# Output banks added up in memory by transfers, and spread between the last chunks of a stage

## The chip, the cores and the metric

The kernel runs on one NeuronCore of a Trainium2 chip. The core has five engines that run at the same time, each its own list of instructions in order: TensorE multiplies matrices (PE in the profile, PEld for its loads of weights), VectorE (DVE), ScalarE (ACT) and GpSimd (POOL) work element by element, and SyncE (SP) starts transfers between the chip's memory and the on-chip memory. Sixteen DMA engines carry these transfers. TensorE writes its results into eight PSUM banks of 128 partitions by 512 floats, and a bank is free again when another engine has read it. The metric is the device time of one execution in microseconds (us). Before the change the median of three runs is 953.04 us (951.15 to 953.58).

## The reference

A windowed attention (4 batches, 8 heads, 576 positions, each looking at 64 positions) makes 2304 tokens of 512 numbers; two gated layers follow. In the second, which the change touches, both factors are linear:

```
x = attention(q, k, v)                          # 2304 x 512
x = (sigmoid(x @ w_gate) * (x @ w_val)) @ w_out   # 512 -> 1536 -> 512
a, b = x @ w_a, x @ w_b                         # 2304 x 1536 each
out = (a * b) @ w_out2                          # 2304 x 512
```

The weights come as 64-bit floats; the result is 32-bit.

## The kernel before, in words

Tokens go in nine blocks of 256. The hidden width of 1536 goes in twelve chunks of 128 (`fc` from 0 to 11). Every factor of a product is kept as a high and a low part, and a product is three matmuls: high by high, high by low, low by high.

The stage around the change is the second layer for tokens 0 to 1279, from about 375 to 580 us; it is followed by the first layer for tokens 1280 to 2303. Tokens 256 to 1279 are a group of four blocks. For each chunk `quad` (L915, with its matmuls in `multiply`, L849) computes both factors by seven products instead of eight, whose sums ScalarE keeps as `r` (L868) and VectorE adds (L871); VectorE then multiplies the factors (L881), and ScalarE and VectorE split the result into `hh` and `hl` or the two parts of `h` (L481, L483). Block 0, tokens 0 to 255, is computed plainly, chunk by chunk, by `hidden` (L507, matmuls L472): chunks 0 to 5 during the stage, 9 to 11 at its end, 6 to 8 later. Its own output is added up by `projection` (matmuls L525, VectorE's add L597).

After every second chunk, a *pair*, `row_banks` (L1106) makes the output of the four blocks: eight banks of 128 tokens by 512 columns (name `accq`, matmuls L987), each the sum of 12 matmuls with one PSUM bank. Six pairs make 48 banks of work. The first pair's banks are copied by ScalarE into four tiles `resf` on chip (L989), those of the other five are added to these by VectorE (L991), and with the last pair SyncE writes the result (L1122). PSUM has two banks for this (`ps_acc`), so the third bank of work waits until the first has been read.

The banks aren't made at once: each is a job in a list `rest`, and `fill(n)` runs the next n jobs. During a quad some jobs run between the products; at the stage's end `fill(3)` and `fill(len(rest))` stand behind block 0's three chunks. A scheduler then orders each engine's instructions by an estimate of its own, within the dependencies and some that are put in by hand (`in_order`, `paced`).

Beside this run two more streams. Weights of the coming chunks are decoded from 64-bit words (L373 to L401 on ScalarE, VectorE and GpSimd), combined for the seven products by GpSimd (`s`, `wq`, L422, L430), and saved to memory by SyncE (`ka`, `kb`, `ko`, L365, and `kq`, L432). At the end the operands of the next stage are loaded back (`xq`, from `bx`, L1193) and split by ScalarE (`op`, L797) and VectorE (L798, with sums L805), and its first weights are loaded (`wf`, L830) and combined by GpSimd (L450, L453).

Of the kernel before, what the change touches and what calls it, by code (L numbers as in the profile page):

```python
# [10 lines left out]
F32 = mybir.dt.float32  # L11
# [4 lines left out]
ALU = mybir.AluOpType  # L16
# [5 lines left out]
def tile_window_attention_gated_mlps(ctx, tc, q, k, v, w1g, w1v, w1o, w2a, w2b, w2o, out):  # L22
    nc = tc.nc
# [3 lines left out]
    P = 128  # L27
# [1074 lines left out]
    def fill(n=1):  # L1102
        for _ in range(min(n, len(rest))):
            rest.pop(0)()

    def row_banks(res, hs, rows, begin, end):  # L1106


        banks = []
        for i in range(2 * NP):  # L1110
            j, sl = i // NP, slice(i % NP * P, (i % NP + 1) * P)
            cols = (slice(0, CH), slice(CH, W)) if end and rows[0] > N and i == 2 * NP - 1 else (slice(0, W),)
            r0 = rows[j] + i % NP * P
            for c in cols:
                pairs = [(h[j][a][:, sl], o[b][:, c]) for o, h in hs for a, b in ((0, 0), (0, 1), (1, 0))]
                banks.append((pairs, res[i // 2][:, i % 2, c], out[r0:r0 + P, c]))
        for pairs, d, to in banks:

            def job(d=d, p=pairs, b=begin, to=to):
                bank_sum(d, p, b)  # L1120
                if end:
                    nc.sync.dma_start(out=to, in_=d)  # L1122

            rest.append(job)
        return banks

    x_ops = next(built)
    fill(len(rest))
    x_ops = next(built)
# [15 lines left out]
                    i, at, mybir.DependencyInfo(mybir.DependencyClass.NoSync, mybir.DependencyReason.DATA), reason="paced"  # L1145
                )

    hs, h0s, res = [], [], None
    seconds = (
        lambda: late["hs"].tile([P, 2, W], F32R, tag="hs", name="h1"),  # L1150
        lambda: wts.tile([P, 2, DM], F32R, tag="wa", name="h1"),
# [2 lines left out]
    for fc in range(NF):  # L1154
        alone = ALONE.get(fc, ())
        for i, f0 in enumerate(alone):
            need(NF + f0, NEVER)
            w = parts[NF + f0]
            h0s.append((w, hidden(1, w, x[1, (0,)])))
            fill(2)  # L1160
            if i == len(alone) - 1:
                rest.append(lambda a=(1, 0, h0s, fc == 0, False): projection(*a))
                h0s = []
        need(NF + fc, NEVER)
        if fc == NF - 1:
            eased = len(nc.cur_bb.bb.instructions)
        limit[0] = min(NW - 1, NF + fc + 2)
        if fc == 0:
            res = [accp.tile([P, 2, W], F32, tag="xacc", name=f"resf{i}") for i in range(4)]
        w = parts[NF + fc]  # L1170
        g = [tmp.tile([P, W], F32, tag="hr", name=f"g{i}") for i in range(2)]
        counts = ((0, 0, 1, 1, 1, 1, 0), (0, 0, 1, 1, 1, 1, 0)) if len(rest) <= 4 else ((0, 1, 1, 1, 1, 1, 1), (0, 1, 1, 1, 1, 1, 1))
        extra = max(0, len(rest) - sum(counts[0]))

        def between(i):
            fill(counts[0][i] + (extra if i == 4 else 0))
            for _ in range(((0, 0, 0, 0, 2, 2, 2) if fc == 0 else (1, 1, 1, 0, 1, 1, 1))[i]):
                paced()

        hs.append((w["o"], quad(1, w, x_ops, between, g, seconds[fc % 3], lambda: None)))  # L1180
        if len(hs) == PAIR:
            fill(len(rest))
            row_banks(res, hs, (3 * N, N), fc == PAIR - 1, fc == NF - 1)
            hs = []
    late.clear()
    middle.close()
# [9 lines left out]
    for fc in BETWEEN:  # L1196
        h0s.append((parts[NF + fc], hidden(1, parts[NF + fc], x[1, (0,)])))
        x_ops = next(built)
    in_order(eased, (mybir.EngineType.DVE,))
    rest.append(lambda a=(1, 0, h0s, False, False): projection(*a))  # L1200
    steps = [(0, fc) for fc in range(NF)] + [(None, fc) for fc in LATER] + [(1, fc) for fc in range(NF)]
    fetched = []
# [1 line left out]
    def ahead(n):  # L1204
        while len(fetched) <= min(n, len(steps) - 1):
            ph, fc = steps[len(fetched)]
            fetched.append(fetch((1 if ph is None else ph) * NF + fc, ph is None))

    tied = len(nc.cur_bb.bb.instructions)
    ahead(0)  # L1210
    fill(3)
    whole(built)
    fill(len(rest))
    SLOTS = {4: (1, 0, 1, 0, 1, 1, 0), 7: (0, 1, 1, 1, 2, 1, 1)}

    def slots(number, first=False):
# [126 lines left out]
```

## Time and profile before

| | us |
|---|---|
| median of three runs | 953.04 |
| the profiled execution | 955.45 |
| its span, first to last instruction | 953.5 |
| TensorE busy in the span | 925.9 |
| VectorE busy | 708.4 |
| ScalarE busy | 478.8 |
| GpSimd busy | 303.3 |

Busy times are shares of one span, and engines work side by side, so they aren't added. The time is set by the chain of waits that ended last, and an engine's idle time counts only where that chain runs through it. In the rows below, `<-` behind an instruction in brackets names what ended the idle time before it; a name on the left of `<-` is what is written, on the right what is read.

### The profile page before, as it was taken

To read this page: it belongs to the slowest core of one execution; us is meant where nothing else is said; L and a number is where in the kernel's file an instruction comes from. 1 tells how busy PE (TensorE), PEld (TensorE's weight loads), DVE (VectorE), ACT (ScalarE), POOL (GpSimd) and SP (SyncE) were. 2 spreads that over 40 slices of the span, in tenths; PEclk is the share of its full clock that TensorE was granted. 3 is DMA by queue.
4 is the path that set the end of the run, shared out by engine and by line. 5 is a ranking of instruction groups with operands and counts; after the bars stand their busy time and mean duration, and the time that the engine had idled before them with its cause. 6 is when DMAs were issued, how large, how long until landed. Compare 5 with 4: busy or idle time off the path is not lost.

```text
span 953.5 us, 15652 instructions
## 1 busy us (share of the span) xinstructions
PE 925.9 (97%) x5504; PEld 773.1 (81%) x5504; DVE 708.4 (74%) x1379; ACT 478.8 (50%) x1063; POOL 303.3 (32%) x321
## 2 busy tenths in 40 slices
PE   7899999999999999999999989999999999999998
PEld 6698888887887788778877777788888888888886
DVE  6998787786569799788999875778788773354445
ACT  7897555686744456564555534655444243211111
POOL 4543222343226714362655336544430000000000
PEclk9999999999999999999999999999999999999999
DMA  8987598988568626565877566354547675554212
GB/s 203 237 237 221 197 326 291 336 286 245 153 220 310 225 109 220 195 220 178 269 236 261 210 198 222 111 188 158 158 150 220 198 275 153 159 173 134 89 66 88
DMA packets 144685, 193.69 MB, mean 203 GB/s; under 512 B 63584, under 2 KB 98912, under 8 KB 143968
## 3 DMA queue, kind: packets, MB, share of 16 engines
q1 hardware_dynamic: 144608, 192.71, 62.5%
q8 instruction: 43, 0.70, 0.3%
q14 instruction: 34, 0.28, 0.1%
HBM read 118.75 MB, written 69.47 MB: 197 GB/s over the span
## 4 chain that ended last, share of the span: by engine, by line
PE 69%; DVE 14%; DMA 5%; POOL 4%; ACT 4%; issue 3%; SPq 0%; DVEq 0%; POOLq 0%; ACTq 0%
PE qa L849 16%; PE accq L987 11%; PE qb L849 8%; PE gps L472 7%; PE vps L472 6%; PE accm L573 6%; PE qc L849 4%; PE accy L950 3%; PE accx L950 2%; DVE ex L392 2%; DVE wi L382 2%; PE xps L228 2%; DVE wi L379 1%; DVE wi L386 1%; DMA st_o<-in_moe_w_out_dram 1%
## 5 line engine op out<-in xcount | busy, mean ns | idle before, releaser
L849 PE MATMUL qa<-op,wq 128*128 128x512 f32 x432 | 112.9, 391 | 2.7 <-ACT r L868 2.3
L849 PE MATMUL qb<-op,wq 128*128 128x512 f32 x432 | 110.7, 390 | 0.9 <-POOL wq L430 0.6
L868 ACT ACTIVATE r<-qa 128x512 f32<-128x512 f32 x108 | 62.5, 594 | 90.0 <-PE qa L849 88.8
L472 PE MATMUL vps<-xh,wb 128*128 128x256 f32 (+1 forms) x392 | 105.6, 338 | 0.2 <-ACT hr L496 0.2
L472 PE MATMUL gps<-xh,wa 128*128 128x256 f32 (+1 forms) x392 | 105.2, 338 | 0.0
L849 PEld LDWEIGHTS qa<-op,wq 128*128 128x128 f32 x432 | 80.9, 188 | 20.4 <-ACT r L868 3.0
L849 PEld LDWEIGHTS qb<-op,wq 128*128 128x128 f32 x432 | 81.0, 188 | 18.4 <-POOL wq L430 1.0
L573 PE MATMUL accm<-hh,wo 128*128 128x512 f32 (+1 forms) x296 | 85.6, 357 | 1.6 <-DVE gacc L550 1.3
L386 POOL TENSOR_TENSOR wi<-wi,low 128x512 int32<-128x512 int32 x36 | 50.1, 1393 | 113.2 <-DVE wi L382 78.3
L472 PEld LDWEIGHTS gps<-xh,wa 128*128 128x128 f32 x392 | 69.2, 191 | 8.5 <-DVE hl L483 0.3
L472 PEld LDWEIGHTS vps<-xh,wb 128*128 128x128 f32 x392 | 69.0, 190 | 8.0 <-ACT hr L496 0.4
L987 PE MATMUL accq<-wo,h 128*128 128x512 f32 (+1 forms) x300 | 71.2, 382 | 3.8 <-DVE resf L991 3.7
L987 PEld LDWEIGHTS accq<-wo,h 128*128 128x128 f32 x300 | 54.8, 188 | 15.8 <-DVE resf L991 4.7
L472 PE MATMUL gps<-xl,wa 128*128 128x256 f32 (+1 forms) x196 | 65.9, 336 | 0.5 <-DVE xl L237 0.5
L472 PE MATMUL vps<-xl,wb 128*128 128x256 f32 (+1 forms) x196 | 65.7, 335 | 0.0
L392 DVE SCALAR_TENSOR_TENSOR ex<-ex,wi 128x512 f32<-128x512 f32 x72 | 53.3, 741 | 14.6 <-ACT ex L376 7.4
L481 ACT ACTIVATE hh<-qa 128x512 fp32r<-128x512 f32 x36 | 21.5, 597 | 84.4 <-DVE qa L881 55.5
L573 PEld LDWEIGHTS accm<-hh,wo 128*128 128x128 f32 x296 | 52.9, 189 | 11.9 <-DVE gacc L550 4.0
L987 PE MATMUL accq<-wo,hh 128*128 128x512 f32 x184 | 56.3, 397 | 1.5 <-ACT hh L481 1.4
L849 PE MATMUL qa<-op,wb 128*128 128x512 f32 x216 | 55.2, 391 | 1.9 <-ACT r L868 1.9
L849 PE MATMUL qc<-op,wa 128*128 128x512 f32 x216 | 56.9, 390 | 0.0
L189 ACT ACTIVATE pr<-pr,stat 128x128 f32<-128x128 f32 x144 | 54.0, 391 | 5.4 <-DVE stat L183 5.2
(180 smaller groups left out, 2154.9 us busy)
## 6 DMA issues: line engine op xcount, KB each, us to landing
wo<-ko SPq DMA_DIRECT2D x27, 512.0 KB, 4.2
wa<-ka SPq DMA_DIRECT2D x27, 512.0 KB, 4.4
st_o<-in_moe_w_out_dram SPq DMA_DIRECT2D x24, 512.0 KB, 5.0
ka<-wa SPq DMA_DIRECT2D x24, 512.0 KB, 5.4
kb<-wb SPq DMA_DIRECT2D x24, 512.0 KB, 3.9
ko<-wo SPq DMA_DIRECT2D x24, 512.0 KB, 5.1
kq<-wq SPq DMA_DIRECT2D x48, 256.0 KB, 4.5
wq<-kq SPq DMA_DIRECT2D x48, 256.0 KB, 3.2
```

What stands on the lines that cost most here:

```text
L189: nc.scalar.activation(out=pr[e][:, j, :], in_=pr[e][:, j, :], func=AF.Exp, bias=nmax[:, e, j:j + 1], scale=-1.0, accum_out=None if t in O ...
L228: nc.tensor.matmul(xps[dims, j, rows], lhsT=vv[:, 2 * j + e, :], rhs=pt[e][:, j, rows], start=True, stop=True)
L382: nc.vector.scalar_tensor_tensor(out=wi, in0=w1, scalar=-(1 << 30), in1=wi, op0=ALU.bitwise_and, op1=ALU.bitwise_or)
L386: (nc.vector if F >= NF else nc.gpsimd).tensor_tensor(out=wi, in0=wi, in1=low, op=ALU.add)
L392: nc.vector.scalar_tensor_tensor(out=wf, in0=wf, scalar=SMALLEST, in1=wi.bitcast(F32), op0=ALU.is_ge, op1=ALU.mult)
L472: nc.tensor.matmul(ps, lhsT=a[:, c * P:(c + 1) * P], rhs=b[:, c, :], start=(n == 0), stop=(n == 3 * NP - 1))
L481: nc.scalar.activation(out=hh, in_=hr, func=AF.Copy, scale=factor)
L573: nc.tensor.matmul(ps[:, m], lhsT=a[:, sl], rhs=b, start=k == 0, stop=k == total - 1)
L849: nc.tensor.matmul(ps, lhsT=a[:, c * P:(c + 1) * P], rhs=b[:, c, :], start=first and n == 0, stop=n == 5, skip_group_check=True,)
L868: nc.scalar.activation(out=r[n], in_=ps, func=AF.Copy)
L950: nc.tensor.matmul(bank[k], lhsT=a[n][i][:, sl], rhs=b[n][j], start=start and m == 0, stop=m == 2, skip_group_check=True,)
L987: nc.tensor.matmul(ps, lhsT=a, rhs=b, start=n == 0, stop=n == len(pairs) - 1)
```

## The change

The banks of tokens 256 to 1279 are no longer added up on chip. A new function `added_rows` takes the place of `row_banks` in this stage: ScalarE copies each bank into half of a tile `added`, of which a ring of buffers is used, and each full tile (256 tokens by 512 columns) is sent to the output. For the first pair SyncE writes it; for the other five GpSimd issues a transfer that adds it to what stands in memory. A tile is sent when the next tile's first bank has been multiplied, and the last one as a job of its own. VectorE's adds and the writes at the end are gone.

At the stage's end three jobs follow each of block 0's chunks 9, 10 and 11, and the rest comes ahead of the remaining operands of the next stage.

```diff
@@ -1124,6 +1124,41 @@
             rest.append(job)
         return banks
 
+    def added_rows(hs, rows, begin):
+
+
+        for i in range(2 * NP):
+            j, sl = i // NP, slice(i % NP * P, (i % NP + 1) * P)
+            pairs = [(h[j][a][:, sl], o[b]) for o, h in hs for a, b in ((0, 0), (0, 1), (1, 0))]
+            r0 = rows[j] + (i % NP - 1) * P
+
+            def job(i=i, p=pairs, to=out[r0:r0 + 2 * P].rearrange("(a p) f -> p a f", p=P) if i % 2 else None):
+                if i % 2 == 0:
+                    added[0] = accp.tile([P, 2, W], F32, tag="xacc", name="added")
+                bank_sum(added[0][:, i % 2], p, True)
+                if i % 2 == 0 and unsent:
+                    unsent.pop()()
+                if i % 2:
+                    unsent.append(lambda t=added[0]: send(t, to, begin))
+
+            rest.append(job)
+        rest.append(lambda: unsent.pop()())
+
+    unsent = []
+
+    def send(t, to, begin):
+        if begin:
+            nc.sync.dma_start(out=to, in_=t)
+        else:
+            at = next(i.name for i in reversed(nc.cur_bb.bb.instructions) if i.engine == mybir.EngineType.PE)
+            since = len(nc.cur_bb.bb.instructions)
+            nc.gpsimd.dma_start(out=to, in_=t, accum_op=ALU.add)
+            for i in nc.cur_bb.bb.instructions[since:]:
+                tc.add_manual_dep(
+                    i, at, mybir.DependencyInfo(mybir.DependencyClass.NoSync, mybir.DependencyReason.DATA), reason="send"
+                )
+
+    added = [None]
     x_ops = next(built)
     fill(len(rest))
     x_ops = next(built)
@@ -1145,7 +1180,7 @@
                     i, at, mybir.DependencyInfo(mybir.DependencyClass.NoSync, mybir.DependencyReason.DATA), reason="paced"
                 )
 
-    hs, h0s, res = [], [], None
+    hs, h0s = [], []
     seconds = (
         lambda: late["hs"].tile([P, 2, W], F32R, tag="hs", name="h1"),
         lambda: wts.tile([P, 2, DM], F32R, tag="wa", name="h1"),
@@ -1165,8 +1200,6 @@
         if fc == NF - 1:
             eased = len(nc.cur_bb.bb.instructions)
         limit[0] = min(NW - 1, NF + fc + 2)
-        if fc == 0:
-            res = [accp.tile([P, 2, W], F32, tag="xacc", name=f"resf{i}") for i in range(4)]
         w = parts[NF + fc]
         g = [tmp.tile([P, W], F32, tag="hr", name=f"g{i}") for i in range(2)]
         counts = ((0, 0, 1, 1, 1, 1, 0), (0, 0, 1, 1, 1, 1, 0)) if len(rest) <= 4 else ((0, 1, 1, 1, 1, 1, 1), (0, 1, 1, 1, 1, 1, 1))
@@ -1180,7 +1213,7 @@
         hs.append((w["o"], quad(1, w, x_ops, between, g, seconds[fc % 3], lambda: None)))
         if len(hs) == PAIR:
             fill(len(rest))
-            row_banks(res, hs, (3 * N, N), fc == PAIR - 1, fc == NF - 1)
+            added_rows(hs, (3 * N, N), fc == PAIR - 1)
             hs = []
     late.clear()
     middle.close()
@@ -1196,7 +1229,7 @@
     for fc in BETWEEN:
         h0s.append((parts[NF + fc], hidden(1, parts[NF + fc], x[1, (0,)])))
         x_ops = next(built)
-    in_order(eased, (mybir.EngineType.DVE,))
+        fill((3,3,3)[fc - BETWEEN[0]])
     rest.append(lambda a=(1, 0, h0s, False, False): projection(*a))
     steps = [(0, fc) for fc in range(NF)] + [(None, fc) for fc in LATER] + [(1, fc) for fc in range(NF)]
     fetched = []
@@ -1206,11 +1239,11 @@
             ph, fc = steps[len(fetched)]
             fetched.append(fetch((1 if ph is None else ph) * NF + fc, ph is None))
 
+    in_order(eased, (mybir.EngineType.DVE,))
     tied = len(nc.cur_bb.bb.instructions)
     ahead(0)
-    fill(3)
+    fill(len(rest))
     whole(built)
-    fill(len(rest))
     SLOTS = {4: (1, 0, 1, 0, 1, 1, 0), 7: (0, 1, 1, 1, 2, 1, 1)}
 
     def slots(number, first=False):
```

TensorE's order at the stage's end. `accq` is a bank of the last pair, `gps` and `vps` are the two factors of a plain chunk of block 0, and `acc` is its projection. Before:

```order
L472 MATMUL vps_6919<-xh1_0_4715,wb_6513 128x256
L987 MATMUL accq_6990<-wo_6422,hh_6698 128x512 x2
L987 MATMUL accq_6990<-wo_6422,hl_6699 128x512
L987 MATMUL accq_6990<-wo_6566,hh_6779 128x512 x2
L987 MATMUL accq_6990<-wo_6566,hl_6780 128x512
L987 MATMUL accq_7007<-wo_6422,hh_6698 128x512 x2
L987 MATMUL accq_7007<-wo_6422,hl_6699 128x512
L987 MATMUL accq_7007<-wo_6566,hh_6779 128x512 x2
L987 MATMUL accq_7007<-wo_6566,hl_6780 128x512
L987 MATMUL accq_7016<-wo_6422,h1_6726 128x512 x3
L987 MATMUL accq_7016<-wo_6566,h1_6791 128x512 x3
```

After, at the second and third of block 0's chunks:

```order
L472 MATMUL vps_6944<-xh1_0_4715,wb_6348 128x256
L987 MATMUL accq_6969<-wo_6457,hh_6741 128x512 x2
L987 MATMUL accq_6969<-wo_6457,hl_6742 128x512
L987 MATMUL accq_6969<-wo_6594,hh_6815 128x512 x2
L987 MATMUL accq_6969<-wo_6594,hl_6816 128x512
L472 MATMUL gps_6995<-xh1_0_4715,wa_6522 128x256
L472 MATMUL gps_6995<-xl1_0_4716,wa_6522 128x256
L472 MATMUL gps_6995<-xh1_0_4715,wa_6522 128x256 x2
L472 MATMUL gps_6995<-xl1_0_4716,wa_6522 128x256
L472 MATMUL gps_6995<-xh1_0_4715,wa_6522 128x256 x2
L472 MATMUL gps_6995<-xl1_0_4716,wa_6522 128x256
L987 MATMUL accq_6978<-wo_6457,h1_6762 128x512 x3
```

Six banks stood behind the last chunk before, one after the other; now two stand ahead of the first chunk, three singly between the chunks, and three behind the last.

SyncE's order of transfers near the end of the weight decoding. `xq` are the operands of the next stage, `k...` are saves of weights of chunks 10 and 11. Before:

```order
L365 DMA ko22_231<-wo_6422 128x1024
L365 DMA ka23_233<-wa_6494 128x1024
L1193 DMA xq01_6820<-bx1_140 128x1024
L1193 DMA xq00_6816<-bx0_139 128x1024
L365 DMA kb23_234<-wb_6513 128x1024
L432 DMA kq11_263<-wq5_6549 128x512
L432 DMA kq11_263<-wq6_6551 128x512
L1193 DMA xq11_6822<-bx1_140 128x1024
```

After:

```order
L432 DMA kq11_263<-wq5_6577 128x512
L432 DMA kq11_263<-wq6_6579 128x512
L432 DMA kq11_263<-wq7_6581 128x512
L432 DMA kq11_263<-wq3_6583 128x512
L365 DMA ko23_235<-wo_6594 128x1024
L1226 DMA xq01_6856<-bx1_140 128x1024
L1226 DMA xq00_6852<-bx0_139 128x1024
L1226 DMA xq11_6858<-bx1_140 128x1024
L1226 DMA xq10_6854<-bx0_139 128x1024
```

The four loads of `xq` stood between the last saves, the first two of them ahead of `kb23`; now all four stand behind the last save, `ko23`.

GpSimd's order from the last decoded weight to the first sums of the next stage, after:

```order
L401 TENSOR_TENSOR wo<-ex,wo 128x512
L1155 DMA out_dram<-added 128x2x512 x5
L450 TENSOR_TENSOR s_7060<-wf 128x256
L450 TENSOR_TENSOR s_7065<-s_7060,wf 128x256
L450 TENSOR_TENSOR s_7070<-wf 128x256
```

Before, L450 came directly behind L401; now five issues of adding transfers stand between them.

## Rows read from the trace of the kernel before

**Rows 1.** Page, busy time of each engine (us, share of the span, instructions)

```profile
PE 925.9 (97%) x5504; PEld 773.1 (81%) x5504; DVE 708.4 (74%) x1379; ACT 478.8 (50%) x1063; POOL 303.3 (32%) x321
```

**Rows 2.** Windows: stretch, length, busy per engine, clock, DMA share, GB/s

```profile
434.00:577.00 143.00, 137.11 (x642) 112.77 (x641) 129.03 (x196) 72.20 (x136) 63.88 (x68) 1.00 0.65 219
```

**Rows 3.** Windows of 20 us, same columns

```profile
520.00:540.00 20.00, 18.85 (x81) 14.67 (x81) 19.06 (x29) 10.63 (x21) 9.82 (x10) 1.00 0.70 245
540.00:560.00 20.00, 20.00 (x108) 17.33 (x107) 15.14 (x22) 5.80 (x9) 0.00 (x0) 1.00 0.47 166
560.00:580.00 20.00, 15.73 (x88) 12.86 (x88) 15.40 (x20) 7.83 (x16) 14.74 (x16) 1.00 0.59 203
```

**Rows 4.** Waits of PE, 434 to 600: us in total, times, longest us

```profile
PE accq L987 <- DVE resf L991: 3.7, 2, 2.5
PE qa L849 <- ACT r L868: 1.4, 2, 0.7
PE qb L849 <- POOL wq L430: 0.6, 1, 0.6
PE qa L849 <- DVE g L871: 0.6, 1, 0.6
PE accq L987 <- ACT hh L481: 0.6, 1, 0.6
PE acc L525 <- DVE resf L991: 0.4, 1, 0.4
PE qb L849 <- DVE hl L483: 0.3, 1, 0.3
PE vps L472 <- ACT hr L496: 0.2, 1, 0.2
```

**Rows 5.** Timeline of PE: start, us, instruction [idle before]

```profile
569.85 4.41 PE L987 MATMUL accq<-wo,h 128*128 128x512 f32 x18 [2.48 <-DVE resf L991]
...
575.45 1.70 PE L987 MATMUL accq<-wo,h 128*128 128x256 f32 x12 [1.20 <-DVE resf L991]
...
577.55 0.73 PE L525 MATMUL acc<-wo,hh 128*128 128x512 f32 x2 [0.40 <-DVE resf L991]
```

**Rows 6.** Groups by line, 375 to 625: count, busy, mean ns, idle before

```profile
L991 DVE TENSOR_TENSOR resf<-accq,resf 128x512 f32<-128x512 f32 (+1 forms) x41 | 26.7, 667 | 2.1 <-PE accq L987 2.0
...
L401 POOL TENSOR_TENSOR wo<-ex,wo 128x512 fp32r<-128x512 f32 x10 | 13.6, 1361 | 20.3 <-ACT wo L398 20.2
...
L989 ACT ACTIVATE resf<-accq 128x512 f32<-128x512 f32 x8 | 4.6, 594 | 2.8 <-PE accq L987 2.8
```

**Rows 7.** Timelines of ACT and PE around 545 us

```profile
544.38 1.06 ACT L797 ACTIVATE op<-xq 128x1024 fp32r<-128x1024 f32 x1 [3.54 <-DMA xq<-bx]
...
547.20 1.52 PE L849 MATMUL qa<-op,wb 128*128 128x512 f32 x6
```

**Rows 8.** Timeline of SP's issues, and the landing of xq

```profile
537.87 0.38 SPq L1193 DMA_DIRECT2D xq<-bx  x1
...
539.97 0.32 SPq L365 DMA_DIRECT2D ko<-wo  x1
...
DMA to landing us min/median/max: 3.8/5.9/6.8
```

**Rows 9.** Timeline of POOL, 530 to 574 us

```profile
530.05 0.74 POOL L422 TENSOR_TENSOR s<-ex 128x256 f32<-128x256 f32 x1 [7.45 <-DVE ex L392]
...
561.41 0.73 POOL L450 TENSOR_TENSOR s<-wf 128x256 f32<-128x256 f32 x1 [21.47 <-DMA wf<-kf]
...
573.67 4.08 POOL L453 TENSOR_TENSOR wq<-s,wq 128x256 fp32r<-128x256 f32 x3
```

**Rows 10.** Page, DMA queue of SP: packets, MB, share of 16 engines

```profile
q1 hardware_dynamic: 144608, 192.71, 62.5%
```

**Rows 11.** Timeline of DVE at the stage's end

```profile
577.75 1.77 DVE L805 TENSOR_TENSOR t<-xq,t 128x1024 f32<-128x1024 f32 x1
```

## The prediction

> **What bounds the kernel now.** I read the page's busy shares first: TensorE works 97% of the span and its clock is at the full 2.4 GHz almost throughout, so only its idle time can be won [rows 1]. Next the windows over the stage that the change touches. From 434 to 577 us, in which all but the last few of the adds that it removes run, TensorE is idle 143 − 137.1 = 5.9 us, while VectorE is busy 129.0 of 143, ScalarE 72.2, GpSimd 63.9 and the DMA engines 0.65 [rows 2]. By pieces, TensorE's largest hole is from 560 to 580: 4.3 of 20 us [rows 3]. Then the waits of TensorE alone: from 434 to 600 they sum to 7.8 us, of which 3.7 + 0.4 are for VectorE's add of an output bank, four waits of 0.3 to 0.6 (2.1 together) come before 555 us, and 1.4 us belongs to the next stage [rows 4]. The timeline shows the 4.1 us one by one: 2.48, 1.20 and 0.40 us, all while the last banks wait for a free PSUM bank, which VectorE gives back only after its adds, and those stand behind preparing the next stage's operands [rows 5]. So the stage is bound by TensorE, with VectorE close to full beside it, and at its end by VectorE.
>
> **The change, part by part.**
>
> *Removed: VectorE's adds.* 41 instructions (40 banks, one of them in two halves), 26.7 us in all, go from VectorE [rows 6]. This stands beside TensorE's work except at the end, where it makes the 4.1 us of waits. There banks now stand between block 0's chunks, so they are no longer crowded behind them, and each needs only a ScalarE copy. I take all three waits as gone. The last bank, whole again, takes a third of the 4.41 us of three whole ones, 1.47, for the 1.70 of its twelve half-width matmuls [rows 5]: 0.2 us. Sum: −4.3 us; bounds 0 (another wait takes their place) to −4.3.
>
> *Earlier in the stage* the four waits of 2.1 us (for g, for hl, for hh and for wq) are each for a result that is VectorE's or depends on its decoding [rows 4]. With 26 of its 129 us gone, some of them end sooner; which ones the trace doesn't say. I take half, −1.0 us; bounds 0 and −2.1.
>
> *Added: 40 ScalarE copies.* A copy of a bank took 594 ns [rows 6], so 23.8 us come onto 72.2 of 143, 67% after it. What stands behind a copy on ScalarE is r (L868), for which TensorE waits already, and hh. One copy ahead of an r can cost at most its 0.6 us. Most of these are hidden by the other PSUM bank; I take +0.3, bounds 0 and +2.
>
> *Added: 20 adding transfers issued by GpSimd, and 4 plain ones by SyncE.* No transfer is issued by GpSimd in the trace. From below, a SyncE issue took 0.32 us [rows 8]; from above, GpSimd's longest ordinary instruction, L401, took 1.36 us [rows 6]. So 6 to 27 us come onto GpSimd's 63.9 of 143. It has waits that hide this: 7.45 us before its sums at 530, 21.47 us before the first of the next stage at 561 [rows 9]. The order puts five issues in that long wait; at 1.36 us each they take 6.8 us, and the last of them needs only the first two banks of the last pair, which stand ahead of block 0's first chunk. I take 0; bounds 0 and the third rival.
>
> *Added: DMA work.* A transfer is 128 × 2 × 512 floats, 0.524 MB. SyncE's queue moved 192.71 MB in 62.5% of the engines' span of 953.5 us, so 0.524 MB takes 1.62 us of all sixteen [rows 10]. If the adding costs nothing more, 20 of them take 32 us; on 0.65 × 143 = 93 us that is 126 of 143, a share of 0.88. That fits, and no engine waits for a weight word in the stage before. I take 0 on the path; the upper bound is the second rival.
>
> *Moved: the loads of xq.* SyncE now issues all four behind the last four saves of kq and the save of ko; before, the last of them was issued at 537.87 and ko at 539.97 [rows 8]. ScalarE already waited 3.54 us for one of them, at 544.38 [rows 7], and TensorE wasn't held up then: it is busy 20.00 of 20 us from 540 to 560 [rows 3]. With ko at 540 and 0.38 us for each issue, the last load is issued at 541.5 and, at the median of 5.9 us [rows 8], lands at 547.4. The second L797 (1.06) and a bank's copy (0.59) end at 549.1. By the new order TensorE wants that copy for the seventh bank of its pair, just ahead of the quad's product with wb, which started at 547.20 [rows 7]: a stall of 1.9 us, or 2.8 if it lands after the longest 6.8. But the decoding that ko ends hangs on VectorE, which is freer, so ko should come sooner. I take +1.0, between 0 and 2.8.
>
> *Sum.* −4.3 − 1.0 + 0.3 + 1.0 = −4.0 us. The profiled execution took 955.45 us (span 953.5 and 1.95 around it), 2.4 more than the median of the three runs shown, 953.04. So 951.4 for its like, and 949.0 for a median.
>
> **The rivals.**
>
> *A wait on ScalarE takes the place of the one removed.* The xq loads come as late as worked out above, so the stall is 2.8 us and not 1.0, and the earlier waits stay, because their cause is the fixed order of decoding and products: −4.3 + 0.3 + 2.8 = −1.2, so 951.8. For it speaks that ScalarE does wait for xq before [rows 7], and that it now releases every PSUM bank of this stage. Against it: 5.80 of 20 us busy from 540 to 560 leave it room to catch up [rows 3].
>
> *Slower: the adding transfers fill the DMA engines.* To add, an engine must read the row in memory as well as write it. If that doubles its time, a transfer takes 3.25 us of all engines, 20 take 65, and 93 + 65 = 158 us don't fit into 143. The stage then runs at the pace of its loads and stretches by 15 us: 953.0 + 15 − 4.0 = 964.0. It decides from (143 − 93) / 20 = 2.5 us of a transfer on; a little above that, the time is near the one before. First signs would be late weight words, and ScalarE's copy waiting for the transfer that still reads its buffer, four tiles earlier. Against it: the share of 0.65 counts saves that nobody waits for [rows 2], and these can queue. On this, the Trainium skill ("Collectives: The Full Stack", "The bandwidth ceiling: the fold count and why AG ≠ RS ≠ AR") says that an adding transfer between cores is slow because it needs two source reads, and measured a ratio of 1.93 to a copy; by that ratio this rival's time would come out. No row here shows an adding transfer.
>
> *GpSimd becomes late.* If each issue waits for an instruction of VectorE to leave a shared path, the longest at the stage's end is L805's, 1.77 us [rows 11]; 1.4 + 1.8 = 3.2 us an issue, 64 us for 20, and GpSimd is at 128 of 143. One sign of such a thing is there: three L453 took 4.08 us at 573.67 beside VectorE's wide instructions, where a like GpSimd instruction took 0.74 at 530.05 [rows 9]. Then wq of a quad comes a microsecond late, nine times: +9 − 4.0, 958.0. The Trainium skill states this ("SBUF — State Buffer", "SBUF: two separate sides"): while VectorE runs an instruction in a mode with two ports, GpSimd can't write the descriptors of a transfer that it issues. By that rule the change would have been better with issues from another engine.
>
> *More than forecast.* All 2.1 us of the earlier waits go and nothing new comes: 953.0 − 4.3 − 2.1 − 0.6 for the same relief of the next stage's first products = 946.0.
>
> **How the numbers follow.** The forecast holds with 0.50, in its own range of 946.5 to 951.5. The first rival has 0.20, the DMA rival 0.15, GpSimd's 0.06, more than forecast 0.09. A difference under 0.3%, 2.9 us, can't be told from none here, so faster means under 950.2 and slower over 955.9. The forecast gives 0.43 to faster and 0.07 to the same; more than forecast 0.09 to faster; the first rival 0.17 to the same and 0.03 to slower, since its stall can grow under the new traffic; the DMA rival 0.04 to the same and 0.11 to slower; GpSimd's 0.06 to slower. That is 0.52, 0.28 and 0.20. The range of 945 to 957 leaves out the heavy part of the DMA rival and a thin end below.
>
> **What would show it.** Right: from 560 to 580 TensorE has no wait for a bank, its wait list names no VectorE add of this stage, and VectorE's share falls from 0.90 to about 0.72. The copies (48 of them, 0.59 us each) run without a wait for a transfer, and GpSimd's issues end before its first sum of the next stage. The xq term: ScalarE's wait before L797 around 545 us, and TensorE's wait for a bank or r right after it; over 3 us there, or the earlier 2.1 us still there, means the first rival. Adding transfers that take more than 2.5 us of all engines, weight words that land late, or copies that wait for a transfer mean the second. Issues over 3 us on GpSimd and TensorE waiting for wq mean the third. The forecast is wrong if the four microseconds at the stage's end are still there under another name.

## The result and the profile after

The changed kernel takes 963.45 us (median of four runs, 962.67 to 963.88) against 952.62 for the kernel before on the same chip: a ratio of 1.0114, 95% interval 1.0097 to 1.0132. It is 10.8 us slower; 949.0 was forecast. The profiled execution took 962.67 us, its span 960.9, 7.4 more than the span before.

The page of the changed kernel, busy times and GpSimd's DMA queue (packets, MB, share of 16 engines), beside [rows 1, 10]:

```profile
PE 928.0 (97%) x5498; PEld 774.0 (81%) x5498; DVE 694.5 (72%) x1338; ACT 498.0 (52%) x1103; POOL 328.4 (34%) x341
...
q0 software_dynamic: 5440, 10.49, 6.9%
```

VectorE lost its 41 adds but only 13.9 us of busy time, where 26.7 were expected [rows 6]. The transfers by GpSimd account for 4.3 us of that shortfall: in the run below that leaves them out, VectorE is busy 690.2 us. Why the other 8.5 are missing stays open. An adding transfer took 0.069 × 960.9 / 20 = 3.3 us of all sixteen DMA engines, twice the 1.62 that SyncE's queue takes for as many bytes [rows 10].

Windows of the changed kernel (length, busy per engine, granted clock, DMA share, GB/s), beside [rows 2, 3]:

```profile
434.00:577.00 143.00, 134.66 (x610) 109.73 (x609) 108.71 (x146) 84.20 (x161) 79.40 (x79) 0.99 0.95 255
520.00:540.00 20.00, 15.52 (x59) 11.68 (x58) 15.82 (x20) 11.58 (x22) 14.77 (x15) 0.91 0.96 277
540.00:560.00 20.00, 20.00 (x91) 16.61 (x90) 7.71 (x11) 9.43 (x14) 4.81 (x4) 1.00 0.97 208
580.00:600.00 20.00, 17.64 (x64) 13.65 (x65) 11.28 (x12) 8.18 (x16) 15.36 (x18) 0.83 0.97 286
```

VectorE's share fell from 0.90 to 0.76, the DMA share rose from 0.65 to 0.95, and TensorE is idle longer, not shorter. The granted clock is 0.91 and 0.83 where it was 1.00: for a part of these stretches the matmuls run at the lower of the clock's two levels, 1.2 GHz instead of 2.4. That loses 0.09 × 20 + 0.17 × 20 = 5.2 us. The kernel before had lost some of this kind too, earlier in the stage, where the changed one lost none. The stretch from 375 to 434, before and after:

```profile
375.00:434.00 59.00, 55.79 (x275) 46.76 (x274) 48.70 (x71) 34.22 (x68) 29.00 (x28) 0.97 0.66 231
...
375.00:434.00 59.00, 55.92 (x288) 47.16 (x287) 48.82 (x74) 35.40 (x72) 30.13 (x28) 1.00 0.78 273
```

That is 0.03 × 59 = 1.8 us of the kernel before, so the clock costs the changed kernel 3.4 us more.

Waits of TensorE from 434 to 600 (us in total, times, longest), beside [rows 4], and the holes one by one, beside [rows 5]:

```profile
PE qa L849 <- ACT r L868: 4.7, 2, 3.7
PE acc L525 <- ACT added L989: 3.8, 2, 2.4
PE accq L987 <- DVE xacc L597: 2.8, 2, 1.5
PE accq L987 <- ACT added L989: 1.4, 2, 0.9
PE qb L849 <- DVE qc L871: 0.2, 1, 0.2
```

```profile
458.29 0.73 PE L987 MATMUL accq<-wo,hh 128*128 128x512 f32 x2 [1.45 <-DVE xacc L597]
...
532.61 2.29 PE L849 MATMUL qa<-op,wq 128*128 128x512 f32 x6 [3.73 <-ACT r L868]
...
579.88 0.74 PE L525 MATMUL acc<-wo,hh 128*128 128x512 f32 x2 [2.37 <-ACT added L989]
...
582.25 1.22 PE L525 MATMUL acc<-wo,hh 128*128 128x512 f32 x2 [1.39 <-ACT added L989]
```

No wait of the banks for L991 is left, and 3.8 us for the copies stand in its place. The waits sum to 12.9 us, 5.1 more than before; over the wider stretch from 375 to 640 they are 16.6 against 11.0, 5.6 more. With the 3.4 us of slow clock that is 9.0. At the start of the stage this execution was 2.4 us ahead (the same product with `wb` starts at 377.75 and 380.12) and its span ended 7.4 us longer, so 9.8 us were lost, of which these two terms are 9.0.

Both large holes end on ScalarE. Its timeline at the two places:

```profile
528.84 0.42 ACT L427 ACTIVATE wq<-s 128x256 fp32r<-128x256 f32 x1 [0.42 <-POOL s L422]
529.97 0.42 ACT L427 ACTIVATE wq<-s 128x256 fp32r<-128x256 f32 x1 [0.72 <-POOL s L422]
531.10 0.42 ACT L427 ACTIVATE wq<-s 128x256 fp32r<-128x256 f32 x1 [0.71 <-POOL s L422]
531.42 0.65 ACT L376 ACTIVATE ex<-st_o 128x512 f32<-128x512 f32 x1
531.98 0.58 ACT L868 ACTIVATE r<-qa 128x512 f32<-128x512 f32 x1
...
578.93 0.42 ACT L452 ACTIVATE wq<-s 128x256 fp32r<-128x256 f32 x1 [0.53 <-POOL s L450]
579.25 0.58 ACT L989 ACTIVATE added<-accq 128x512 f32<-128x512 f32 x1
```

At 532 the r for which TensorE waits stands behind three L427 of the next chunk's weights, and each of these waits for GpSimd. In the kernel before the r of this product stood ahead of them:

```profile
528.83 0.59 ACT L868 ACTIVATE r<-qa 128x512 f32<-128x512 f32 x1
...
530.82 0.42 ACT L427 ACTIVATE wq<-s 128x256 fp32r<-128x256 f32 x1 [0.18 <-POOL s L422]
```

At 579 a copy stands behind L452, which waits for GpSimd's sum of the next stage's weights.

GpSimd and VectorE, one of the places where GpSimd issues a transfer:

```profile
442.36 1.36 POOL L1155 DMA_DIRECT2D out_dram<-added  x1 [0.31 <-ACT added L989]
443.43 3.12 POOL L430 TENSOR_TENSOR wq<-s,wq 128x256 fp32r<-128x256 f32 x4
...
443.64 3.47 DVE L382 SCALAR_TENSOR_TENSOR wi<-st_o,wi 128x512 int32<-128x512 int32 x1
```

L382 never took more than 1.61 us in this stage before. It took 2.34, 2.69 and 3.47 us here, each time while GpSimd issued a transfer or ran what stood directly behind one.

### The profile page after: what moved, and what is told of

Read it like the earlier page. It is cut to its first block, busy times and chain, and to the rows that moved or that the text cites. A ratio compares the mean times of both kernels' runs of the same rounds, so it can differ in the third digit from the quotient of the medians.

```text
span 960.9 us, 15689 instructions
## 1 busy us (share of the span) xinstructions
PE 928.0 (97%) x5498; PEld 774.0 (81%) x5498; DVE 694.5 (72%) x1338; ACT 498.0 (52%) x1103; POOL 328.4 (34%) x341
## 4 chain that ended last, share of the span: by engine, by line
PE 71%; DVE 12%; DMA 5%; ACT 4%; POOL 4%; issue 3%; SPq 0%; DVEq 0%; POOLq 0%; ACTq 0%
PE qa L849 16%; PE accq L987 11%; PE qb L849 8%; PE gps L472 7%; PE vps L472 7%; PE accm L573 6%; PE qc L849 4%; PE accy L950 3%; PE accx L950 2%; DVE ex L392 2%; DVE wi L382 2%; PE xps L228 2%; DVE wi L386 1%; DVE wi L379 1%; PE sps L170 1%
## 5 line engine op out<-in xcount | busy, mean ns | idle before, releaser
L392 DVE SCALAR_TENSOR_TENSOR ex<-ex,wi 128x512 f32<-128x512 f32 x72 | 54.8, 761 | 15.2 <-ACT ex L376 7.5
L987 PEld LDWEIGHTS accq<-wo,h 128*128 128x128 f32 x294 | 54.3, 188 | 12.9 <-ACT added L989 1.8
L573 PEld LDWEIGHTS accm<-hh,wo 128*128 128x128 f32 x296 | 52.9, 189 | 10.8 <-DVE gacc L550 2.8
L453 POOL TENSOR_TENSOR wq<-s,wq 128x256 fp32r<-128x256 f32 x48 | 39.4, 843 | 53.0 <-ACT wq L452 52.9
```

The source lines that it names most:

```text
L392: nc.vector.scalar_tensor_tensor(out=wf, in0=wf, scalar=SMALLEST, in1=wi.bitcast(F32), op0=ALU.is_ge, op1=ALU.mult)
L453: nc.gpsimd.tensor_tensor(out=t[:, 1], in0=s, in1=t[:, 0].bitcast(F32), op=ALU.subtract)
L573: nc.tensor.matmul(ps[:, m], lhsT=a[:, sl], rhs=b, start=k == 0, stop=k == total - 1)
L987: nc.tensor.matmul(ps, lhsT=a, rhs=b, start=n == 0, stop=n == len(pairs) - 1)
```

## The experiments

Three causes were tried. **A**: the adding, or the traffic, fills the DMA engines. **B**: the order of ScalarE's list and the new end. **C**: GpSimd's issuing beside VectorE, which later expectations split: by itself (C1) or by waits in GpSimd's list (C2), and of C1 by issues (C1a) or by any instruction (C1b). Medians, and ratios to the kernel before on the same chip; the kernels ran on several chips, so below two of them are compared by how far each is above the kernel before on its own chip:

| kernel | us | ratio, 95% interval |
|---|---|---|
| changed, plain writes by GpSimd | 964.49 | 1.0116 (1.0091 to 1.0141) |
| changed, no transfers by GpSimd | 957.28 | 1.0042 (1.0024 to 1.0060) |
| changed, end of before | 962.14 | 1.0093 (1.0068 to 1.0118) |
| before, new end | 963.30 | 1.0111 (1.0082 to 1.0140) |
| changed, plain writes by SyncE | 956.20 | 1.0035 (1.0024 to 1.0045) |
| copies alone | 955.81 | 1.0025 (1.0010 to 1.0040) |
| changed, r ahead of the decoding | 960.14 | 1.0075 (1.0056 to 1.0093) |
| changed, copies ahead of L452 | 964.45 | 1.0116 (1.0096 to 1.0136) |
| changed, source always ready | 965.85 | 1.0135 (1.0104 to 1.0166) |
| before, 19 transfers by GpSimd | 965.18 | 1.0136 (1.0108 to 1.0165) |
| before, 19 transfers by SyncE | 953.11 | 1.0003 (0.9991 to 1.0015) |
| before, last pair by transfers | 954.72 | 1.0025 (1.0011 to 1.0039) |
| before, 19 additions on GpSimd | 957.87 | 1.0052 (1.0033 to 1.0070) |
| copies alone, r ahead | 952.02 | 0.9989 (0.9975 to 1.0003) |

**Plain writes in place of adding ones.**

```diff
-            nc.gpsimd.dma_start(out=to, in_=t, accum_op=ALU.add)
+            nc.gpsimd.dma_start(out=to, in_=t)
```

> The changed kernel with GpSimd's 20 transfers writing instead of adding: same order on every engine, same issues, and the sums over the pairs are left out. Theory A, the adding itself fills the DMA engines (3.3 us of all sixteen per transfer, share 0.95 from 434 to 577): a plain one takes 1.6 us, the share falls to about 0.85, the wait of 3.7 us for r at 532 and its slow clock go, and with them most of the loss: 951 to 955 us. Theory B, the order that the copies, GpSimd's issues and the spread end bring: nothing of it is changed, so 961 to 964 us, with the waits of 2.4 and 1.4 us at 580 still there. Theory C, GpSimd's issuing beside VectorE stretches both: GpSimd still issues all 20, so 961 to 964 us, and a decoding instruction L382 of over 2 us is still seen.

It took 964.49 us. GpSimd's queue and the window of the stage in this kernel:

```profile
q0 software_dynamic: 2880, 10.49, 2.8%
```

```profile
434.00:577.00 143.00, 135.62 (x616) 110.81 (x615) 107.47 (x148) 84.87 (x163) 73.56 (x79) 0.99 0.73 256
```

The DMA share went back from 0.95 to 0.73, and the time did not move. A falls: full DMA engines were not what this stage ran at.

**No transfers by GpSimd.**

```diff
-        else:
+        elif False:
             at = next(i.name for i in reversed(nc.cur_bb.bb.instructions) if i.engine == mybir.EngineType.PE)
```

> The changed kernel with the 20 transfers of GpSimd left out (the first pair is still written by SyncE; the sums over the pairs are left out). The copies and the order of TensorE and ScalarE stay. Theory A (the adding fills the DMA engines): 950 to 954 us, the DMA share from 434 to 577 near 0.65. Theory B (order): 958 to 962 us, since the end still has ScalarE's L452 ahead of the copies of banks. Theory C (GpSimd's issuing): 950 to 954 us as for A, but then the run with plain transfers must have stayed over 960.

957.28 us, 4.1 above the kernel before (953.23), where the changed kernel is 10.8 above: the transfers cost some 6.8 us and what is left 4. The wait for r near 531 is still there, 2.96 us, so it isn't theirs; that was in favour of B.

**The stage's end as before, and the new end alone.** The second kernel is the kernel before with the reverse of this edit.

```diff
-        fill((3,3,3)[fc - BETWEEN[0]])
+    in_order(eased, (mybir.EngineType.DVE,))
...
-    in_order(eased, (mybir.EngineType.DVE,))
...
-    fill(len(rest))
+    fill(3)
     whole(built)
+    fill(len(rest))
```

> The changed kernel with the stage's end of the kernel before: no bank between block 0's three chunks, three banks and then the rest behind them as before; copies and adding transfers stay. Theory B (order): the waits of 2.4 and 1.4 us at 580 and the half clock behind them, about 3.4 us, go, so 955 to 958 us. Theory A (the adding fills the DMA engines) and C: the transfers are all still there, so 961 to 965 us, with waits at the end for other late things.

> The kernel before with the new end of the stage alone: VectorE still adds the banks on chip, no adding transfers, but three jobs follow each of block 0's last chunks. Theory B (order): wf is loaded later and the banks get in each other's way, so slower than the kernel before by 2 to 6 us: 955 to 959 us. Theory A and C: nothing of theirs is in it, so the same as before or some 1 to 3 us less, 950 to 953 us.

962.14 and 963.30 us. With the old end the changed kernel has one wait of 3.61 us for a copy in place of 2.37 and 1.39, and the time hardly moves: B's forecast for it was wrong. The new end alone loses nearly as much as the whole change. VectorE there, and TensorE's wait:

```profile
571.36 1.64 DVE L798 TENSOR_TENSOR op<-t,op 128x1024 fp32r<-128x1024 f32 x1 [2.91 <-ACT op L797]
572.92 1.28 DVE L991 TENSOR_TENSOR resf<-accq,resf 128x512 f32<-128x512 f32 x2
```

```profile
PE accq L987 <- DVE resf L991: 8.6, 3, 3.9
```

The adds stand behind L798, which waits for ScalarE, and 8.6 us of waits replace 4.1. The clock costs more than these 4.5 us:

```profile
560.00:580.00 20.00, 14.09 (x53) 10.97 (x51) 10.95 (x14) 5.84 (x13) 14.69 (x16) 0.74 0.57 188
580.00:600.00 20.00, 16.65 (x69) 13.65 (x70) 8.73 (x12) 6.03 (x11) 4.12 (x7) 0.91 0.59 200
```

That is 0.26 × 20 + 0.09 × 20 = 7.0 us at places where the kernel before has 1.00. So the two parts of the change don't add up: the new end is only bearable with copies. With copies and no transfers the two ends are 4.1 and 2.9 us above the kernel before (957.28 and 955.81), a difference that these runs hardly tell from nothing.

**Plain writes by SyncE.**

```diff
-            nc.gpsimd.dma_start(out=to, in_=t, accum_op=ALU.add)
+            nc.sync.dma_start(out=to, in_=t)
```

> The changed kernel with its 20 transfers issued by SyncE, as plain writes (the sums over the pairs are left out). So far: 963.5 with adding transfers from GpSimd, 964.5 with plain ones from GpSimd, 957.3 with none; adding costs nothing more on the path, but something about the sends costs 6 to 7 us. Theory A', the traffic does it (late landings of other loads and saves): the bytes are the same, so 961 to 965 us. Theory C, GpSimd's issuing does it (1.2 us each on GpSimd, and beside it VectorE's L382 took up to 2.7 us): with SyncE issuing, 955 to 959 us, as without sends, and GpSimd's instructions between 434 and 577 back to 63 us.

956.20 us, 3.3 above the kernel before (952.88). The same plain writes issued by GpSimd are 11.3 above (953.23), so they cost 8 us more, and SyncE's no more than leaving them out: who issues is what costs. The queue goes with the issuer, so no run parts the two. The clock is back:

```profile
520.00:540.00 20.00, 16.42 (x72) 12.93 (x71) 15.53 (x23) 11.60 (x23) 10.71 (x10) 1.00 0.76 280
...
580.00:600.00 20.00, 18.53 (x81) 14.72 (x80) 12.61 (x15) 10.82 (x21) 14.25 (x16) 1.00 0.61 208
```

**A source that is always ready.** GpSimd's list waits 37 us for copies in the changed kernel; here it doesn't. The transfers read an operand of block 0.

```diff
-            nc.gpsimd.dma_start(out=to, in_=t, accum_op=ALU.add)
+            nc.gpsimd.dma_start(
+                out=to, in_=x[1, (0,)][0].rearrange("p (a b) n -> p a (b n)", a=2).bitcast(F32), accum_op=ALU.add
+            )
```

> The changed kernel with the same 20 adding transfers from GpSimd at the same places, but read from an operand of block 0 that is always ready, in place of the copied banks (which then go nowhere; the output isn't the sum). GpSimd's list has no more waits for ScalarE's copies (37 us in the changed kernel). Theory C1, the issuing itself costs the 7 us (24 us of GpSimd and VectorE's instructions stretched beside it: every L382 over 2 us overlaps an issue): 961 to 965 us. Theory C2, the waits in GpSimd's list in front of the sums of weights cost it: 955 to 958 us, as with SyncE.

965.85 us, 12.8 above the kernel before (953.07): the waits in GpSimd's list are not the cause.

**The issues alone, on the kernel before.** In `row_banks` every second of VectorE's adds of this stage gets a transfer beside it, by GpSimd and in a second kernel by SyncE; nobody waits for its data.

```diff
+                if not b and rows == (3 * N, N) and d.shape[-1] == W and len(sent) < 39:
+                    sent.append(d)
+                    if len(sent) % 2 == 0:
+                        nc.gpsimd.dma_start(
+                            out=spare[len(sent) // 2 % 4],
+                            in_=x[1, (0,)][0].rearrange("p (a b) n -> p a (b n)", a=2).bitcast(F32),
+                        )
```

> The kernel before, VectorE's adds and its end unchanged, with 19 transfers of the same size added that GpSimd issues beside the adds of pairs 2 to 6: they write an operand that is always ready into memory that nobody reads. Theory C1 (issuing by GpSimd costs by itself): slower than the kernel before by 3 to 8 us, 956 to 961 us, since VectorE is even fuller here (129 of 143 us), and L382s of over 2 us are seen. Theory C2 (only waits in GpSimd's list cost): 952 to 954 us.

> The same 19 transfers into memory that nobody reads, added to the kernel before, issued by SyncE. Theories C1 and C2 both: 952 to 954 us, as before, and no L382 over 1.8 us. Theory A' (traffic): as slow as the one with GpSimd.

965.18 and 953.11 us: 19 issues from GpSimd cost 12 us, more than expected, and the same 19 from SyncE nothing. The pages of the two, first GpSimd's, then SyncE's:

```profile
PE 928.6 (96%) x5504; PEld 775.5 (80%) x5504; DVE 717.6 (74%) x1379; ACT 479.0 (50%) x1063; POOL 312.9 (32%) x340
```

```profile
PE 923.9 (97%) x5504; PEld 771.4 (81%) x5504; DVE 708.1 (74%) x1379; ACT 479.1 (50%) x1063; POOL 306.1 (32%) x321
```

VectorE runs the same 1379 instructions and takes 9.5 us longer. Where they go, in GpSimd's and VectorE's timelines of the first:

```profile
480.00 0.73 POOL L422 TENSOR_TENSOR s<-ex 128x256 f32<-128x256 f32 x1 [6.79 <-DVE ex L392]
480.69 0.57 POOL L1128 DMA_DIRECT2D spare<-xh  x1
481.29 0.75 POOL L422 TENSOR_TENSOR s<-s,ex 128x256 f32<-128x256 f32 x1
481.99 0.74 POOL L422 TENSOR_TENSOR s<-ex 128x256 f32<-128x256 f32 x1
482.68 0.73 POOL L422 TENSOR_TENSOR s<-ex,s 128x256 f32<-128x256 f32 x1
483.38 2.10 POOL L430 TENSOR_TENSOR wq<-s,wq 128x256 fp32r<-128x256 f32 x3
...
480.94 5.09 DVE L401 TENSOR_TENSOR wb<-ex,wb 128x512 fp32r<-128x512 f32 x1
```

L401 on VectorE, 0.7 to 1.2 us elsewhere, begins while the issue runs and ends 0.5 us after the last of six further GpSimd instructions. VectorE is held for the whole run. The same happens at 536 (L379, 4.69 us) and 580 (L805, 4.16 us), and TensorE's longest wait of that kernel in the stage, 4.52 us at 542.64, is for a result behind the second. Only a few of the 19 issues do this. But all eight kernels in which GpSimd issues transfers have a VectorE instruction of over 2 us in this stage, and none of the other eight has one. A part of the 12 us is again the clock behind the holes, 0.17 × 20 + 0.09 × 20 = 5.2 us in the profiled run:

```profile
540.00:560.00 20.00, 17.36 (x66) 14.19 (x67) 12.84 (x20) 6.49 (x11) 4.59 (x7) 0.83 0.81 294
...
580.00:600.00 20.00, 15.32 (x65) 12.28 (x64) 15.61 (x15) 7.10 (x13) 16.76 (x18) 0.91 0.76 277
```

**Additions on GpSimd in place of the issues.**

```diff
-                        nc.gpsimd.dma_start(
-                            out=spare[len(sent) // 2 % 4],
-                            in_=x[1, (0,)][0].rearrange("p (a b) n -> p a (b n)", a=2).bitcast(F32),
-                        )
+                        nc.gpsimd.tensor_tensor(out=spare[0], in0=spare[0], in1=spare[0], op=ALU.add)
```

> The kernel before with 19 additions of a small tile (128x256, not used by anything) on GpSimd, at the places where the transfers into unread memory stood that cost 12 us; no transfers. Theory C1a, issuing a transfer is what locks VectorE out of a run of GpSimd instructions (in that kernel one VectorE instruction took 5.09 us, the whole run of GpSimd behind an issue): here no VectorE instruction over 2 us and 952 to 955 us. Theory C1b, any further GpSimd instruction next to the sums of weights does it: 958 us or more, with VectorE instructions of 3 to 5 us again.

957.87 us, between the two forecasts. No VectorE instruction takes 2 us, and VectorE's total is 708.4, as in the kernel before: the long holds belong to issues of transfers. But 19 additions of 0.80 us still cost 5 us, with waits for `wb`, h and banks that the kernel before doesn't have, and a clock of 0.87 and 0.96 from 560 to 600. So a part of what the issues cost may simply be more work in GpSimd's list, at places where the weights wait for it. It is hardly all of it: the additions fill that list for 15.2 us, the 19 issues for 10.9, and the issues cost 12. How large a part it is, is not settled, since an addition isn't an issue.

**The copies alone.** The edits of the second and third kernel together: no transfers by GpSimd, and the end of the kernel before.

> The copies alone: the changed kernel without the 20 transfers of GpSimd and with the stage's end of the kernel before (the sums over the pairs are left out). Theory B, the order of ScalarE's list: without VectorE's adds the scheduler puts steps of the weight decoding ahead of r (L868) in ScalarE's list, so the wait of 3 us near 531 stays, with its slow clock, and at the end a copy waits behind L452: 955 to 959 us, slower than the kernel before although VectorE's 26.7 us are gone. Rival, the copies are free and all of the loss is the new end and the sends: 948 to 951 us.

955.81 us, 2.9 more than before although nothing of VectorE's adds is left; the wait for r is 3.00 us. That is B's forecast. In the next two, one with GpSimd's transfers and the new end and one with the copies alone, r stands ahead:

```diff
-            for _ in range(((0, 0, 0, 0, 2, 2, 2) if fc == 0 else (1, 1, 1, 0, 1, 1, 1))[i]):
+            for _ in range(((0, 0, 0, 0, 2, 2, 2) if fc == 0 else (0, 1, 0, 0, 0, 1, 0) if fc == NF - 3 else (1, 1, 1, 0, 1, 1, 1))[i]):
```

> The changed kernel with the last steps of the weight decoding written some products later, so that in ScalarE's list the r (L868) of the quad at 532 stands ahead of the last chunk's L427 and not behind three of them; transfers, copies and the end as they are. Theory B (order): the wait of 3.7 us for r and the fall of the clock behind it, 1.7 us, go; the next quad may wait 1 to 2 us for its weights instead: 958 to 961 us. Theories A and C (traffic or GpSimd's issuing make the decoding late): the wait moves to the same place under the name of a weight, and the time stays at 962 to 965 us.

> The copies alone (no transfers by GpSimd, the end of the kernel before; the sums over the pairs are left out), with the last steps of the weight decoding written later so that r (L868) stands ahead of them on ScalarE. The copies alone took 955.8 us, with 3.0 us of waiting for r at 530. Theory B (the order of ScalarE's list is what the copies cost): the wait goes, 951 to 953.5 us, no slower than the kernel before. Rival, ScalarE's copies cost by themselves: it stays at 955 to 957 us.

960.14 and 952.02 us. The first is 7.3 above the kernel before (952.88), where the changed kernel is 10.8 above: the wait of 3.73 us for r is gone, one of 1.40 us for hh stands near its place, and the clock is 1.00 from 520 to 540. In the second the scheduler's list for ScalarE has r ahead of all four L427 of the last chunk, and TensorE's waits from 434 to 600 are

```profile
PE accq L987 <- ACT added L989: 3.4, 3, 1.5
PE qa L849 <- ACT r L868: 1.8, 3, 0.9
PE accq L987 <- DVE xacc L597: 1.4, 1, 1.4
```

The 3.8 us between the two kernels of copies come with that one edit, which takes away the wait of 3.00 us and, from 520 to 540, a clock of 0.91; it moves other steps of the decoding as well. And with it, leaving out the adds and all their transfers, for 40 more copies by ScalarE, is worth 0.9 us, by the interval no more than 2.4: VectorE's adds cost the kernel before almost nothing more than the copies would.

**Copies ahead of L452.** The L452 of the first fetch get a dependency on the last copy.

```diff
-    ahead(0)
     fill(len(rest))
+    last = next(i.name for i in reversed(nc.cur_bb.bb.instructions) if i.engine == mybir.EngineType.Activation)
+    since = len(nc.cur_bb.bb.instructions)
+    ahead(0)
+    for i in nc.cur_bb.bb.instructions[since:]:
+        if i.engine == mybir.EngineType.Activation:
...
```

> The changed kernel with L452, ScalarE's part of the next stage's first weights, put behind the last copy of a bank in ScalarE's list; the rest as it is. Theory B (order): the waits of 2.4 and 1.4 us at 580 go and with them the half clock behind (3.4 us); the next stage's second product then waits for its weight for 1 to 3 us: 957 to 961 us. Rival, the weights wf are late anyway and bound the next stage's start: the wait only changes its name, 962 to 965 us.

964.45 us, the rival's forecast. TensorE, GpSimd, VectorE and ScalarE there:

```profile
592.82 2.93 PE L849 MATMUL qa<-op,wq 128*128 128x512 f32 x6 [4.27 <-ACT r L868]
...
579.62 1.20 POOL L1155 DMA_DIRECT2D out_dram<-added  x1 [1.34 <-ACT wq L452]
...
581.22 7.63 DVE L798 TENSOR_TENSOR op<-t,op 128x1024 fp32r<-128x1024 f32 x1 [1.32 <-ACT op L797]
...
590.62 1.06 ACT L797 ACTIVATE op<-t 128x1024 fp32r<-128x1024 f32 x1 [5.33 <-DVE t L805]
...
592.19 0.58 ACT L868 ACTIVATE r<-qa 128x512 f32<-128x512 f32 x1
```

The waits for copies at 580 are gone, and 4.27 us appear some ten microseconds later. The r stands behind an L797, which waits for VectorE, and VectorE stands at L798 for 7.63 us (1.2 to 1.7 in the changed kernel) behind GpSimd's last issue, the longest such hold of all runs. So the wait came back through the cost of C, and the time doesn't show that the weights `wf` were late anyway, as the rival has it; what the place of the copies is worth without the issues, this run can't tell.

**A version for gain.** VectorE adds pairs 1 to 5 on chip, SyncE writes them, and only the last pair goes by copies and four adding transfers.

```diff
-            row_banks(res, hs, (3 * N, N), fc == PAIR - 1, fc == NF - 1)
+            if fc == NF - 1:
+                added_rows(hs, (3 * N, N), False)
+            else:
+                row_banks(res, hs, (3 * N, N), fc == PAIR - 1, fc == NF - 1 - PAIR)
```

> A version for gain: the kernel before with VectorE's adds for pairs 1 to 5, written out by SyncE after the fifth, and only the last pair's eight banks by ScalarE copies and four adding transfers from GpSimd; the end in the order of before. If the loss comes from 20 issues by GpSimd beside VectorE's decoding and from copies ahead of r in the stage, this has neither (four issues after the decoding), and of the 4.1 us of waits for VectorE's adds about half go, as in the run with copies alone, where 1.7 us stayed: 950 to 952 us. If the new waits behind L452 are as long as the old: 952 to 954 us; over 955 us would speak for the four sends late in GpSimd's list ahead of the next stage's weights.

954.72 us, 1.7 slower than the kernel before, and not the 950 to 952 that were forecast. TensorE waits 1.87 and 1.48 us for copies where it waited 2.48 and 1.20 for adds [rows 5], and beside the four issues VectorE's L805 took 2.74 and 2.69 us. No version here that still adds up the output beats the kernel before.

## Why the prediction was wrong

Step by step, each against the kernel before on its chip: copies with r ahead −0.9 us, copies alone +2.9, with the new end +4.1, and with GpSimd's adding transfers, the whole change, +10.8.

*GpSimd's issues at 0: the step that failed.* The last of these steps, 6.8 us, was put at 0. The price of one issue was within its bounds (0.32 to 1.36 us; 20 took 24.7 us, 1.24 each), and the long wait did hide five of them. What was not asked is what an issue does to VectorE. Issued by GpSimd rather than SyncE, the plain writes cost 8 us, 19 of them on the kernel before 12. The third rival had the right pair of engines, at 0.06, with the wrong victim: it let GpSimd wait for VectorE, 3.2 us an issue, while the runs show single VectorE instructions held for 2.3 to 7.6 us.

*The Trainium skill on this.* In the trace of the 19 issues VectorE's instruction behind one is stretched (5.09 us) and GpSimd's beside it are not (0.73 to 0.75). The Trainium skill ("SBUF — State Buffer", "SBUF: two separate sides") calls the ports that VectorE and GpSimd share an exclusive lock that the first comer keeps for its whole instruction, and advises to issue from another engine's queue. The advice agrees with the trace (953.11 against 965.18 us). The stall that the section describes for such transfers, GpSimd kept from writing descriptors by VectorE, isn't what these runs show: an issue took 1.20 us at 540.04, with VectorE idle, and 1.19 at 502.02 beside it. And a hold of 5.09 us is longer than any one GpSimd instruction in it (0.75).

*The removed waits at −4.3.* They went, as said, and came back as 3.8 us for copies. "Each needs only a ScalarE copy" overlooked what stands ahead of the copy in ScalarE's list. The forecast's last line named this: the microseconds are there under another name. With the copies alone, r ahead and the end of before, one wait of 1.46 us at 569 stands where 4.1 stood. The first rival was right that a wait on ScalarE would take their place; it laid it to late loads of xq.

*The earlier waits at −1.0 and the copies at +0.3.* The waits for wq, hl and hh are gone, but one r moved behind the decoding, 3.73 us, and xacc, 2.8 us, is new. Putting ScalarE's copies in the place of VectorE's adds came with another order of ScalarE's list; I priced the copies by their length and not by that. With r ahead the copies alone end at 952.0, without at 955.8: +3.8 in place of +0.3, beyond the bound of +2.

*DMA at 0 on the path: right.* A transfer does take 3.3 us, beyond the 2.5 from which the DMA rival was to decide, and the share is 0.95. Yet halving it changed nothing. The reason given, that saves can queue without anyone waiting, fits this, but no run isolates it. That this rival's time, 964.0, is within 1 us of the measured one is luck.

*The move of xq at +1.0* cost nothing: TensorE is busy 20.00 of 20 us from 540 to 560. SyncE issued `ko` at 536.78 and the first xq at 537.93, earlier than the 540 of before, as the prediction thought possible.

*The clock* was in no term. Of the 9.0 us accounted for in the profiled run, 3.4 are the clock: 5.2 us behind the two largest holes, less the 1.8 us that the kernel before had lost earlier in the stage.

## What to carry to other kernels

Before a transfer is moved to GpSimd's queue, look at what VectorE does beside it: on a kernel with VectorE at 0.9 of a stage, 19 issues cost 12 us there and nothing from SyncE. An engine's work is worth what TensorE waits for it: 26.7 us of adds, exchanged for copies, were worth about one, and this can be tried first by leaving the work out. And where a scheduler orders the lists by an estimate, a removed instruction can change the order on other engines; compare the lists around each instruction that TensorE waits for, before its duration is priced.

## What the runs showed of the hardware

- An adding transfer of 0.52 MB from on-chip memory took 3.3 us of all sixteen DMA engines; a plain one from the same queue 0.028 × 960.9 / 20 = 1.35. Its median from issue to landing was 7.3 us against 3.7. The ratio of 1.93 that the Trainium skill gives for adding between cores ("Collectives: The Full Stack", "The bandwidth ceiling: the fold count and why AG ≠ RS ≠ AR") is near the 3.3 / 1.62 = 2.0 against SyncE's plain transfers; against plain ones from the same queue it is 3.3 / 1.35 = 2.5.
- A VectorE instruction that meets an issue of GpSimd can be held through the run of GpSimd instructions behind it (0.7 to 1.2 us became 5.09, and an L798 took 7.63), while GpSimd went on at its usual speed (0.73 to 0.75 us each beside the 5.09).
- The granted clock fell behind holes of 3.7 us in TensorE's work, and behind shorter ones not always. The wait for r near 530 was 2.98 us in the run with SyncE's writes, with the clock at 1.00 from 520 to 540, and 2.96 and 3.00 us in the runs without transfers, with 0.91. A wait for r of 1.89 us at 386 in the kernel before was followed by a fall (0.97 from 375 to 434); the same wait of 1.90 us at 384 in the changed kernel was not (1.00).
